# A planned attention-and-MLP kernel on one core: wq loaded by rows over two queues, Q of the first segment summed chunk by chunk, one filler, a new written-out order, the last store over two queues

## The chip, the cores and the metric

The kernel runs on one core of a Trainium2 chip. Its engines run side by side, each in its own program order: TensorE (PE, with its weight loads shown as PEld) multiplies into PSUM, VectorE (DVE), ScalarE (ACT) and GpSimd (POOL) compute on SBUF and PSUM, and SyncE (SP) issues most of the DMAs; ACT issues a few at the start. They wait for each other and for DMAs by semaphores. The metric is the device time in microseconds of one execution; lower is better. The runs of the kernel before took 265.08, 265.57 and 265.69 us, median 265.57.

## What is computed

The input x has 2048 tokens of width 512. Out comes g * A(x) + (1 - g) * B(x), where g is a sigmoid of a weighted sum of each token. A is an attention with memory over 32 heads of 16 in four segments of 512 tokens, B is a gated MLP of width 1792:

```python
q, k, v = heads(x @ wq), heads(x @ wk), heads(x @ wv)
for s in range(4):                      # segments of 512 tokens
    p = softmax(qs @ ks.T * scale + causal_mask)
    a_dot = p @ vs
    a_mem = (phi(qs) @ M) / (phi(qs) @ z + 1e-6)      # phi(t) = t + 1 if t > 0 else exp(t)
    o[s] = sigmoid(beta) * a_mem + (1 - sigmoid(beta)) * a_dot
    M, z = M + phi(ks).T @ vs, z + phi(ks).sum()
a = o @ wo
b = (relu(x @ W_gate) * (x @ W_up)) @ W_down
out = g * a + (1 - g) * b,  g = sigmoid((x * gate_w).sum(-1))
```

## The kernel before

**Tasks and a written-out order.** The kernel first describes its work as tasks (class `Plan`), each with an engine, a duration that the planner books for it in ns, the tasks that it depends on, and the PSUM banks and ring buffers that it needs and frees. `ORDER` is a list of task numbers and `UNITS` one digit per buffer slot: both were worked out ahead, outside the kernel, from the booked durations and the arrival times in `LANDS` (line 258, ns after the start). In the program they only fix in which order each engine's instructions stand and which bank each task uses. At run time an engine takes its instructions in that order and waits for what it really needs. A DMA issue waits in addition until the DMA eight issues before it, whose semaphore it uses again, has landed.

**The head.** Weights and x come by DMAs issued at the start. The four x tiles of segment 0 (128 tokens each, L266) go alternately over SP and ACT; so do the four 128-row pieces of wq (`load_wq`, L300: even ones on SP, odd ones on ACT). Then SP issues wk in two halves of 256 rows, wv, W_gate and W_up in pieces, gate_w and beta (L308, L310), and the rest. While these come in, PE runs seven matmuls on a constant (`heat`, L911), turns the x tiles (`x0_tasks`, L497: 16 matmuls of 128 columns with an identity, "flips"), whose results DVE and ACT copy from PSUM to xT (L505), and then three fillers (L515) on a tile of zeros.

**Q of segment 0** (`proj_q`, lines 542 to 551): for each of four column groups c, an accumulation in one bank over four row chunks of wq. Chunks 0 and 1 are taken together for the first half of the tokens (256 columns), then together for the second half; chunks 2 and 3 follow with 512 columns. The first half needs the x tiles 0 and 1, the second tiles 2 and 3.

**What follows, per segment.** K and V are projected in the same way (L460 is the helper that records whole matmuls, L464 the same cut into four 32-column parts, which is taken where the array is in that shape already). DVE evicts Q (L556) and K ("ktr", L572), makes masked copies of K ("KT", L575) and phi(K) ("pkT", L529, L530); ACT does the exp for phi (L534). Scores (L623, diagonal blocks L636) of four heads fill the banks 0 to 3, one ACT exp empties them (L645), GpSimd masks the result (L674), and PE multiplies it with V (L696). V is evicted by DVE or ACT (L602). The MLP (`ffn_tasks`) runs between: W_gate and W_up matmuls, relu on ACT (L860), product on DVE (L866, "hT"). `out_tile` sums W_down and wo matmuls into one bank per 128 tokens, DVE scales it (L892) and SP stores it (L897). The last tile is stored in two halves of the columns; its second half is cut into two evictions and one store.

**The head gates.** `head_gates` (lines 382 to 395) is some thirty small DVE instructions that turn beta into per-head factors, after one ACT exp of betab (L395). It is one task, booked with 2000 ns:

```python
got_eb = plan.add("ACT", 200, 0.0, lambda: nc.scalar.activation(
    eb[:], betab[:], ACT.Exp, scale=-1.0), [got_be], 100)
got_gates = plan.add("DVE", 2000, 0.0, head_gates, [got_eb], 100, lock=True)
```

Of the kernel before, what the change touches and what calls it, by code (L numbers as in the profile page):

```python
# [12 lines left out]
P = 128  # L13
# [6 lines left out]
L = S // NSEG  # L20
# [72 lines left out]
"""  # L93

UNITS = (
    "456701230142303000031221111122121222030000003000000010011000002300020000230113110223100023"
    "135121300042016323701290018020d320a211b001c00111002222003003111322000222203122100214567302"
    "1000003300000003201100000200003000001011303031023221103821070016002332053209102a3224113b02"
    "1d213c011211002010120122032121202030212232003145670132000002200000003301100000010000000033"
    "01101302038322101272209312232232036211a0115110b3024103d022c1002120132212242202021113315302"  # L100
    "135671032000002300000002301100000320000000120110238012130303027200901220233212600053214300"
    "a302d024b211c01101200110"
)


class Slot:


    def __init__(self, cands):
        self.cands, self.units, self.left = tuple(cands), (), 0  # L110

    @property
# [66 lines left out]
def kernel(  # L179
# [74 lines left out]
    def work():  # L254
        return plan.one("ps", range(7, -1, -1))


    LANDS = dict(n0=3600, n1=3800, n2=4300, n3=4450, qa=5100, qb=5900, ka=7250, kb=8550, v=10050,
                 g0=11550, u0=13000, gw=14400, be=14650, g1=15900, u1=17250, x1=20700, g2=22000,
                 u2=23100, g3=24200, u3=25300, d0=28100, d1=30800, o=33600)  # L260

# [141 lines left out]
    def K(unit, part=0.0):  # L403
        return unit * UNIT + part
# [572 lines left out]
```

## Time and profile before

| What | Value |
|---|---|
| Median of three runs | 265.57 us (265.08 to 265.69) |
| The profiled execution | 264.89 us, of which the span from first to last instruction is 263.2 us |
| PE busy | 255.8 us, 97% of the span |
| DVE, ACT, POOL busy | 204.4, 183.2, 61.9 us |
| Granted TensorE clock | 1.00 throughout |
| PE busy in 0 to 5.69 us, 5.69 to 22.8, 22.8 to 260.4 | 4.77, 16.27, 234.78 us |
| DVE busy in the same stretches | 1.94, 14.78, 187.36 us |

The span is shorter than the execution's time by what lies before the first and behind the last instruction of the program, 1.69 us. An engine's busy time counts its instructions alone. Matmuls are pipelined, so that the end of one lies behind the start of the next: the step from start to start is what one costs. A few matmul records are missing (28 of 3969 here), so a gap may be one unseen matmul. Chain and waits name who released whom by the semaphores.

### The profile page before, as it was taken

The numbers are of one execution on the slowest core, as the hardware profiler recorded it, in microseconds if no ns is written. First come the engines' busy times: TensorE is split into PE (matmuls) and PEld (weight loads), VectorE is DVE, ScalarE is ACT, GpSimd is POOL, SyncE is SP. The second block draws the span as 40 slices with busy tenths as digits, with TensorE's granted clock in tenths as the row PEclk, the third lists the DMA queues.
The fourth block names the chain that finished last, engine by engine and source line by source line (L and its number), as shares of the span: only waits on it lengthen the run. The fifth ranks groups of instructions, "written<-read, shape, count | busy, mean of one in ns | idle before, by whom it ended". The sixth has DMA issues, their size and how long they took to land.

```text
span 263.2 us, 9091 instructions
## 1 busy us (share of the span) xinstructions
PE 255.8 (97%) x3941; PEld 118.8 (45%) x3969; DVE 204.4 (78%) x473; ACT 183.2 (70%) x168; POOL 61.9 (24%) x168
## 2 busy tenths in 40 slices
PE   8999999999999999999999999999999999999995
PEld 5434444454444444444444444444444444445454
DVE  3799899999655985688998687785999767878722
ACT  3298988899777778878668667788568667873000
POOL 8022622312321322132021222122122223121000
PEclk9999999999999999999999999999999999999999
DMA  6999893011501112002204110022020100041011
GB/s 205 305 254 345 236 221 40 4 22 34 92 17 40 22 32 82 22 12 82 80 4 61 35 24 21 22 94 89 4 80 24 35 4 22 12 146 49 2 42 42
DMA packets 30031, 19.48 MB, mean 74 GB/s; under 512 B 15016, under 2 KB 28456, under 8 KB 29992
## 3 DMA queue, kind: packets, MB, share of 16 engines
q1 hardware_dynamic: 29416, 18.38, 26.0%
q8 instruction: 31, 0.51, 0.8%
q10 hardware_dynamic: 576, 0.52, 0.6%
q14 instruction: 8, 0.07, 0.1%
HBM read 13.21 MB, written 2.55 MB: 60 GB/s over the span
## 4 chain that ended last, share of the span: by engine, by line
PE 90%; DVE 4%; DMA 3%; issue 1%; SPq 0%; DVEq 0%
PE ps L460 48%; PE ps L464 24%; PE ps L623 8%; PE ps L696 7%; DMA wv_sb<-in_A_wv_dram 2%; DMA xn<-in_A_x_dram 1%; PE ps L636 1%; PE ps L816 1%; DVE KT L575 1%; DVE ktr L572 1%; DVE junk L414 1%; PE ps L752 1%; DVE hT L866 0%; DVE gcat L391 0%; PE ps L792 0%
## 5 line engine op out<-in xcount | busy, mean ns | idle before, releaser
L645 ACT ACTIVATE E<-ps 128x2048 bf16<-128x2048 f32 x64 | 120.1, 1876 | 31.3 <-PE ps L623 27.1
L674 POOL TENSOR_SCALAR_AFFINE_SELECT E<-E 128x256 bf16<-128x256 bf16 x128 | 52.6, 435 | 171.5 <-ACT E L645 171.4
L866 DVE TENSOR_TENSOR hT<-ps,rgr 128x512 bf16<-128x512 f32 x56 | 37.6, 678 | 13.4 <-PE ps L460 8.3
L860 ACT ACTIVATE rgr<-ps 128x512 bf16<-128x512 f32 x56 | 33.0, 597 | 14.7 <-PE ps L460 7.3
L460 PE MATMUL ps<-xT,wg_sb 128*128 128x512 bf16 x144 | 40.6, 380 | 1.0 <-issue 0.5
L460 PE MATMUL ps<-wd_sb,hT 128*128 128x512 bf16 (+1 forms) x161 | 37.8, 352 | 0.5 <-issue 0.5
L460 PE MATMUL ps<-xT,wu_sb 128*128 128x512 bf16 x133 | 36.4, 380 | 0.6 <-issue 0.5
L727 DVE STREAM_TRANSPOSE T<-ps 128x512 f32<-128x512 f32 x32 | 22.8, 712 | 12.0 <-PE ps L696 11.8
L623 PE MATMUL ps<-QT,KT 32*128 32x320 bf16 (+3 forms) x512 | 25.4, 273 | 0.0
L892 DVE TENSOR_SCALAR osr<-ps,ngcol 128x512 bf16<-128x512 f32 (+2 forms) x18 | 12.2, 677 | 14.7 <-PE ps L464 8.2
L464 PE MATMUL ps<-xT,wu_sb 128*32 128x512 bf16 x336 | 23.5, 379 | 0.0
L460 PEld LDWEIGHTS <-wg_sb 128*128 128x128 bf16 x152 | 13.9, 98 | 17.7 <-issue 2.4
L460 PEld LDWEIGHTS <-hT 128*128 128x128 bf16 x167 | 14.2, 98 | 16.0 <-issue 2.7
L460 PEld LDWEIGHTS <-wu_sb 128*128 128x128 bf16 x140 | 12.9, 98 | 16.1 <-issue 1.9
L464 PE MATMUL ps<-wd_sb,hT 128*32 128x512 bf16 (+1 forms) x340 | 20.0, 362 | 0.0
L623 PEld LDWEIGHTS <-KT 32*128 32x128 bf16 x512 | 7.6, 92 | 26.4 <-issue 25.9
L696 PE MATMUL ps<-E,Vp 128*17 128x320 bf16 (+3 forms) x512 | 19.5, 274 | 0.0
L464 PE MATMUL ps<-xT,wg_sb 128*32 128x512 bf16 x288 | 19.2, 379 | 0.0
L460 PE MATMUL ps<-xT,wq_sb 128*128 128x512 bf16 (+1 forms) x69 | 17.2, 355 | 0.3 <-issue 0.2
L645 ACT ACTIVATE Em<-ps 128x2048 bf16<-128x2048 f32 x8 | 15.1, 1882 | 3.3 <-PE ps L636 3.3
L460 PE MATMUL ps<-wv_sb,xT 128*128 128x512 bf16 x55 | 15.5, 379 | 0.6 <-DMA wv_sb<-in_A_wv_dram 0.6
L460 PE MATMUL ps<-xT,wk_sb 128*128 128x512 bf16 x50 | 14.3, 380 | 0.1
(102 smaller groups left out, 305.5 us busy)
## 6 DMA issues: line engine op xcount, KB each, us to landing
out_dram<-osr SPq DMA_DIRECT2D x15, 128.0 KB
wd_sb<-in_B_W_down_dram SPq DMA_DIRECT2D x2, 896.0 KB
xn<-in_A_x_dram SPq DMA_DIRECT2D x3, 512.0 KB
cdr<-coefs SPq DMA_DIRECT2D x6, 256.0 KB
xn<-coefs SPq DMA_DIRECT2D x6, 256.0 KB
wg_sb<-in_B_W_gate_dram SPq DMA_DIRECT2D x2, 512.0 KB
wu_sb<-in_B_W_up_dram SPq DMA_DIRECT2D x2, 512.0 KB
wg_sb<-in_B_W_gate_dram SPq DMA_DIRECT2D x2, 384.0 KB
```

Of the source, the lines that this page charges most:

```text
L414: zs.append(plan.add("DVE", 690, key, lambda t=t: nc.vector.scalar_tensor_tensor(junk[:], xn[:, t, :], 1.0, gwb[:], ALU.mult, ALU.mult, ac ...
L460: nc.tensor.matmul(out, lhsT=lhsT, rhs=rhs, start=start, stop=stop)
L464: nc.tensor.matmul(out[r], lhsT=lhsT[:, r], rhs=rhs, start=start, stop=stop, tile_position=(0, 32 * j))
L572: d = plan.add("DVE", 600, key - RQK, lambda: nc.vector.tensor_copy(ktr[ks.i][:], bank(sl)), [a], DVL + 40, need=[ks], frees=[sl])
L623: nc.tensor.matmul(ps[:, j * L + o:j * L + o + L - q], lhsT=KT[i][rows, kb, 3 * r:3 * r + 2].rearrange("p h q -> p (h q)"), rhs=QT[i][rows ...
L645: last_exp[0] = [plan.add("ACT", 66 + 4 * L / 1.2, key, lambda: nc.scalar.activation(dst, ps[:, 0:4 * L], ACT.Exp, scale=SCALE), [a] + war ...
L674: nc.gpsimd.affine_select(out=m[:, :, o:o + HP], in_=m[:, :, o:o + HP], compare_op=ALU.is_ge, fill=0.0, base=HP, pattern=[[0, 4], [1, HP]] ...
L696: nc.tensor.matmul(bank(sl)[32 * m:32 * m + HW, q:q + w], lhsT=(Vp[i] if n < 4 else Vm)[:, kb, r, 4 * c + j, 0:HW], rhs=rhs, start=(n == 0 ...
L727: done.append(plan.add("DVE", 633, key - RL, lambda r=r, sl=sl: nc.vector.transpose(T[ts.i][:, r], bank(sl)), [a] + done, 75 if r else 0, ...
L860: r = plan.add("ACT", 478, key - RL, lambda sl=gsl, rs=rs: nc.scalar.activation(rgr[rs.i][:], bank(sl), ACT.Relu), [g], ACL, frees=[gsl])
L866: nc.vector.tensor_tensor(hT[hs1.i][:], bank(sl), rgr[rs.i][:], ALU.mult)),
L892: nc.vector.tensor_scalar(osr[os.i][:, n0 - c0:n1 - c0], bank(sl)[:, 0:n1 - n0], ngcol[:, tt:tt + 1], None, ALU.mult)),
```

## The change

1. **wq by rows.** The first two chunks of wq (rows 0-127 and 128-255) are each halved by rows, 64 on SP and 64 on ACT, chunk 0 first on both queues. Rows 256 to 511 come in one DMA on SP. So SP issues one transfer more ahead of wk than it did with x and wq, and ACT issues two halves where it issued two whole pieces.
2. **Q of segment 0 chunk by chunk.** Four tasks (chunk 0 first half, chunk 0 second half, chunk 1 first half, chunk 1 second half), each waiting for its own chunk, and then chunks 2 and 3 as before.
3. **One filler** instead of three.
4. **Booked times.** `LANDS` names q0, q1 and qb and moves several arrivals; flips, heat and recall are booked with other durations. The head gates stay at 2000.
5. **A new ORDER and UNITS** for all tasks, from one end of the program to the other. Both programs hold the same matmuls except for two fillers.
6. **The last store** goes half by SP (64 partitions) and half by ACT.

```diff
-    LANDS = dict(n0=3600, n1=3800, n2=4300, n3=4450, qa=5100, qb=5900, ka=7250, kb=8550, v=10050,
-                 g0=11550, u0=13000, gw=14400, be=14650, g1=15900, u1=17250, x1=20700, g2=22000,
+    LANDS = dict(n0=3570, n1=3700, n2=4200, n3=4400, q0=5300, q1=5750, qb=6600, ka=7400, kb=8800,
+                 v=10500, g0=11900, u0=13100, gw=14400, be=14650, g1=15900, u1=17250, x1=20700,
...
-    def load_wq(i):
-        for ci in (2 * i, 2 * i + 1):
-            (nc.scalar if ci % 2 else nc.sync).dma_start(
-                out=wq_sb[:, ci, :], in_=A_wq[ci * P:(ci + 1) * P, :])
-        return arrival("q" + "ab"[i])
-
-    got_q = [load_wq(i) for i in range(2)]
-    got_k = [load_rows(wk_sb, A_wk, i, "k") for i in range(2)]
+    got_q = []
+    for ci in range(2):
+        for n, eng in ((0, nc.sync), (P // 2, nc.scalar)):
+            eng.dma_start(out=wq_sb[n:n + P // 2, ci, :],
+                          in_=A_wq[ci * P + n:ci * P + n + P // 2, :])
+        got_q.append(arrival("q%d" % ci))
+    got_q.append(load_rows(nc.sync, wq_sb, A_wq, 1, "q"))
+    got_k = [load_rows(nc.sync, wk_sb, A_wk, i, "k") for i in range(2)]
...
-            a = plan.add("PE", 107.0 * (c1 - c0), K(-9) + n, flip, [got_n[0][t]], PEL, need=[sl],
+            a = plan.add("PE", 80.0 * (c1 - c0), K(-9) + n, flip, [got_n[0][t]], PEL, need=[sl],
...
-                    for h in range(3):
-                        nc.tensor.matmul(bank(js)[:, 0:2 * P], lhsT=junk[:, 0:P],
-                                         rhs=junk[:, None, 0:P].to_broadcast([P, 2, P]), start=True,
-                                         stop=True)
-                j = plan.add("PE", 640, K(-9) + n + 0.5, idle, [a], lat=0, need=[js], frees=[js],
+                    nc.tensor.matmul(bank(js)[:, 0:2 * P], lhsT=junk[:, 0:P],
+                                     rhs=junk[:, None, 0:P].to_broadcast([P, 2, P]), start=True,
+                                     stop=True)
+                j = plan.add("PE", 320, K(-9) + n + 0.5, idle, [a], lat=0, need=[js], frees=[js],
...
-            for h in range(2):
-                a = matmuls(K(-8 + h, c), [got_q[0]], sl, [
+            for n, (ci, h) in enumerate(((0, 0), (0, 1), (1, 0), (1, 1))):
+                a = matmuls(K(-8 + n, c), [got_q[ci]] + (got_x[0][0] if h else x0_first), sl, [
                     lambda ci=ci, h=h: (wq_sb[:, ci, c * P:(c + 1) * P],
-                                        xT[0][:, ci, h * L // 2:(h + 1) * L // 2])
-                    for ci in range(2)], width=L // 2, at=h * L // 2, prev=a, start=not h, stop=False,
-                    chunk={0: got_x[0][0] if h else x0_first})
-            a = matmuls(K(-6, c), [got_q[1]] + got_x[0][1], sl, proj_mm(wq_sb, c, 0)[2:], prev=a,
+                                        xT[0][:, ci, h * L // 2:(h + 1) * L // 2])],
+                    width=L // 2, at=h * L // 2, prev=a, start=not n, stop=False)
+            a = matmuls(K(-4, c), [got_q[2]] + got_x[0][1], sl, proj_mm(wq_sb, c, 0)[2:], prev=a,
...
-        plan.add("SP", 400, key, lambda: nc.sync.dma_start(
-            out=outf[tt * P:(tt + 1) * P, c0:c1], in_=osr[os.i][:, 0:c1 - c0]), b[-1:],
-            1400 if tt == NT - 1 else 2400, frees=[os], xfer=400.0)
+
+        def store():
+            halves = [(nc.sync, 0, P // 2), (nc.scalar, P // 2, P)]
+            for eng, p0, p1 in halves if c0 else [(nc.sync, 0, P)]:
+                eng.dma_start(out=outf[tt * P + p0:tt * P + p1, c0:c1],
+                              in_=osr[os.i][p0:p1, 0:c1 - c0])
+        plan.add("SP", 400, key, store, b[-1:], 1400 if tt == NT - 1 else 2400, frees=[os],
+                 xfer=400.0)
...
-    plan.add("PE", 3500, -1e9, heat, lat=0, need=warm, frees=warm, size=14)
+    plan.add("PE", 3570, -1e9, heat, lat=0, need=warm, frees=warm, size=14)
```

Where the new order puts things in the first 35 us, engine by engine: PE has all of Q (four column groups) and six of K's matmuls ahead of the first V matmul, where before a part of Q's group 1 stood behind it. The flips go tile by tile (0, 1, 2, 3; before 0, 1, 3, 2), and DVE copies tile 2 ahead of its half of tile 3 (before the other way). DVE has the head gates right behind the eviction of the third K group, ahead of the second V eviction (before they stood behind that group's KT copies and two of the gate sums, L414). ACT has the exp of betab ahead of the second score exp (before behind it).

More of the change, by code (lines that the diff above doesn't have):

```diff
@@ L30 @@
 ORDER = """
[62 rows of a table removed]
[63 rows of a table added]
 """
 UNITS = (
[L96 to L102, printed above, removed]
+    "456701230123406200001221131125111001330000031000000020011000002000000000230112000322100120"
+    "005111322042207113610082239321d111a203b113c01100012323003001001022212222103203230013567013"
+    "2000002300000003301100000200002000021011122200212130123b32342216201331252138211a0037200931"
+    "3d000c120111002220101011222022113032233323000145671230000003200000003301100000310003000011"
+    "0112230402231042213211a32212006122b2038313502391127123d302c1200021121303101222230202210203"
+    "10456213000000330000000220110000000000000070011103301202232112a10311214221631251038022b011"
+    "72039122c514d11000210011"
 )
@@ L255, in work @@
         return plan.one("ps", range(7, -1, -1))
-    LANDS = dict(n0=3600, n1=3800, n2=4300, n3=4450, qa=5100, qb=5900, ka=7250, kb=8550, v=10050,
-                 g0=11550, u0=13000, gw=14400, be=14650, g1=15900, u1=17250, x1=20700, g2=22000,
-                 u2=23100, g3=24200, u3=25300, d0=28100, d1=30800, o=33600)
+    LANDS = dict(n0=3570, n1=3700, n2=4200, n3=4400, q0=5300, q1=5750, qb=6600, ka=7400, kb=8800,
+                 v=10500, g0=11900, u0=13100, gw=14400, be=14650, g1=15900, u1=17250, x1=20700,
+                 g2=22000, u2=23100, g3=24200, u3=25300, d0=28100, d1=30800, o=33600)
     def arrival(name):
@@ L291, in load_x0, with load_rows @@
         return load(eng, xn[:, t, :], x[t * P:(t + 1) * P, :], "n%d" % t)
-    def load_rows(t, ap, i, name):
-        return load(nc.sync, t[:, 2 * i:2 * i + 2, :],
+    def load_rows(eng, t, ap, i, name):
+        return load(eng, t[:, 2 * i:2 * i + 2, :],
                     ap.rearrange("(c p) n -> p c n", p=P)[:, 2 * i:2 * i + 2, :], name + "ab"[i])
     got_n[0] = [load_x0(nc.scalar if t % 2 else nc.sync, t) for t in range(4)]
-    def load_wq(i):
-        for ci in (2 * i, 2 * i + 1):
-            (nc.scalar if ci % 2 else nc.sync).dma_start(
-                out=wq_sb[:, ci, :], in_=A_wq[ci * P:(ci + 1) * P, :])
-        return arrival("q" + "ab"[i])
-    got_q = [load_wq(i) for i in range(2)]
-    got_k = [load_rows(wk_sb, A_wk, i, "k") for i in range(2)]
+    got_q = []
[6 more added lines that the diff above has]
+    got_k = [load_rows(nc.sync, wk_sb, A_wk, i, "k") for i in range(2)]
     got_v = load_cols(nc.sync, wv_sb, A_wv, 0, D, "v")
@@ L513, in idle @@
                 def idle(js=js):
-                    for h in range(3):
-                        nc.tensor.matmul(bank(js)[:, 0:2 * P], lhsT=junk[:, 0:P],
-                                         rhs=junk[:, None, 0:P].to_broadcast([P, 2, P]), start=True,
-                                         stop=True)
-                j = plan.add("PE", 640, K(-9) + n + 0.5, idle, [a], lat=0, need=[js], frees=[js],
-                             size=6)
+                    nc.tensor.matmul(bank(js)[:, 0:2 * P], lhsT=junk[:, 0:P],
+                                     rhs=junk[:, None, 0:P].to_broadcast([P, 2, P]), start=True,
+                                     stop=True)
+                j = plan.add("PE", 320, K(-9) + n + 0.5, idle, [a], lat=0, need=[js], frees=[js],
+                             size=4)
             got.append(b)
@@ L795, in pe @@
                                      tile_position=(32 * j, 32 * m))
-        a = plan.add("PE", 230, key, pe, [prj["pq", seg, c] for c in range(NC)]
+        a = plan.add("PE", 266, key, pe, [prj["pq", seg, c] for c in range(NC)]
                      + [att["mbd", seg - 1]] + [(b, 3900.25) for b in loads], PEL, need=sls,
```

125 rows, old and new, of the table ORDER are left out of this document.

## The prediction

> **What bounds the kernel now.** I read the page first (busy shares, slices, chain), then the timeline of the first 24 us and of the last 25 us.
>
> ```profile
> PE 255.8 (97%) x3941; PEld 118.8 (45%) x3969; DVE 204.4 (78%) x473; ACT 183.2 (70%) x168; POOL 61.9 (24%) x168
> ...
> PE   8999999999999999999999999999999999999995
> PEld 5434444454444444444444444444444444445454
> DVE  3799899999655985688998687785999767878722
> ...
> PE 90%; DVE 4%; DMA 3%; issue 1%; SPq 0%; DVEq 0%
> ```
>
> TensorE is busy in every slice and is 90% of the chain. So the end is the sum of the matmuls plus the few places where PE waits. DVE is nearly as full in the 2nd to 10th slice (6.6 to 66 us): there a PE wait on DVE is likeliest.
>
> ```profile
> 3.57 1.71 PE L497 MATMUL ps<-ident,xn 128*128 128x128 bf16 x16
> 5.12 0.49 PE L515 MATMUL ps<-junk 128*128 128x256 bf16 x3
> 5.69 2.87 PE L460 MATMUL ps<-xT,wq_sb 128*128 128x256 bf16 x18
> ...
> 9.49 0.38 PE L460 MATMUL ps<-xT,wk_sb 128*128 128x512 bf16 x1
> 10.42 0.60 PE L460 MATMUL ps<-wv_sb,xT 128*128 128x512 bf16 x2 [0.55 <-DMA wv_sb<-in_A_wv_dram]
> ```
>
> Read the start times, since ends overlap: from start to start a warm matmul of 512 columns takes 0.216 us, one of 256 columns 0.109. The fillers (L515) are through at 5.45 and the first Q matmul starts at 5.69: 0.25 us of waiting for wq. The second waits until 5.89, 0.09 more (the landings in the trace: wq rows 0-127 at 5.65, rows 128-255 at 5.84). Before the first V matmul one matmul record is missing (0.216), so PE stands from 9.92 to 10.42, 0.50 us, until wv lands (10.37).
>
> ```profile
> 4.24 1.77 DVE L505 CAST xT<-ps 128x512 bf16<-128x512 f32 x3 [2.63 <-PE ps L497]
> ...
> 16.86 0.22 ACT L395 ACTIVATE eb<-betab 128x32 f32<-128x32 bf16 x1
> ...
> 17.53 0.38 DVE L383 TENSOR_SCALAR gall<-eb 128x32 f32<-128x32 f32 x1
> ...
> 20.83 0.68 DVE L866 TENSOR_TENSOR hT<-ps,rgr 128x512 bf16<-128x512 f32 x1
> ...
> 22.77 1.02 PE L460 MATMUL ps<-xT,wg_sb 128*128 128x512 bf16 x4 [0.19 <-DVE hT L866]
> ```
>
> These rows show the head gates (L383 to L393) holding DVE for 3.30 us (17.53 to 20.83), whereas the plan books 2.0 us for them (line 397). PSUM evictions queue behind them, and PE pays about 0.45 us between 21.1 and 22.8. After 22.8 I compared each stretch of matmuls with columns/2.4 GHz plus 0.11 us per change of array shape (as the neighbouring stretches cost) and found no further wait to the end. So from 5.69: 260.33 (last matmul's end) - 5.69 = 254.64, of which 0.09 + 0.50 + 0.45 = 1.04 waits and **253.60 work**.
>
> **The change, part by part.**
>
> *Matmuls.* I counted both programs' PE orders. The column counts weighted by shape differ by 512, which are the two dropped fillers; changes of array shape are 151 in both. 62 fewer records come of 20 matmuls issued whole instead of as four 32-column parts, and four parts cost the same (8 such records, two matmuls, every 0.43 us). So 253.60 holds from the first Q matmul on, whatever the order.
>
> *Start.* The x0 flips end as before (issue done 5.12), one filler to 5.23. wq rows 0-127, now first on both queues, would have landed by 5.65 at the latest if nothing improved; by the bytes in front (640 KB, delivered at 4.28 by the packets, last landings 0.6 to 1.1 us behind packets) at about 5.3. Then four Q matmuls on the first half of the tokens: 4 x 0.109. The fifth needs the second half, hence all of DVE's copies (L505). Their order changes: DVE now copies tile 2 whole (0.69 by the rows) before half of tile 3 (0.43). Tile 2's flips now come before tile 3's and end at 5.06; copies 5.10 to 5.79 and 5.74 to 6.16; matmul at **6.21**. So the start of Q may lie anywhere from 5.35 to 5.77 without moving anything: DVE, not wq, is what comes last. Left from there: 253.60 - 0.44 = 253.16.
>
> *To wv.* Before wv the new order has 12 narrow and 14 wide matmuls from 6.21: 12 x 0.109 + 14 x 0.216 = 4.33, so the first V matmul comes at 10.54; the old order had 0.65 us less work there, and waited. On the way each load must have landed: wq rows 256-511 at 6.97 (one 256 KB transfer, issued at 3.71 as wk's first half was; bytes in front as before, 1024 KB at 5.60, landing about 6.6), wk's halves at 8.60 and 9.03 (before: 7.59 and 8.78), wv 10.54 (10.37), W_gate 12.28 (11.87). I take no wait. Each SP issue behind the added one is 0.4 to 0.5 us later (rows of 0.39 to 0.51 us), but these queues are full: packets of wv end at 9.23, over 4 us after its issue. Bounds: 0, and 0.38 if wv lands 0.5 us later with its issue.
>
> *Behind wv, by rows.* Scores at 11.51 (KT ready 11.19). DVE: Q's chunk 1 to 11.8, pkT, ktr of chunk 2 at 12.48, two KT, V's copy at 13.78, ktr of chunk 1 from 14.63 (its matmuls end 14.60), slot to 15.24. Now the new DVE order puts the head gates here, ahead of the V copy that frees a bank for W_gate piece 1: 15.24 + 3.30 = 18.54, V copy to 19.22, PE released at 19.27. PE gets there at 18.77 (sum of prices): **wait 0.50**. Half-way on, hT1's eviction (end 23.21) holds PE another 0.10. From there I walked DVE and ACT to 34 us (each exp 1.88 us, eviction 0.61 per slot) without finding another. Cost 0.60; bounds 0 (nobody waits) to 0.90.
>
> *The last store.* DVE's final eviction, the issue and the landing lie open at the end:
>
> ```profile
> 260.36 0.35 DVE L892 TENSOR_SCALAR osr<-ps,ngcol 128x128 bf16<-128x128 f32 x1 [0.26 <-PE ps L460]
> ```
>
> The store is issued at 260.74, its packets run 261.57 to 261.92, SP sees it at 262.29. Halving the rows can save at most that packet window's half, 0.17. Against it, in each of the three head pairs issued together (x and wq), ACT's transfer landed 0.19 us after SP's. I take 0; bounds -0.17 to +0.3 (ACT's first packet came 1.51 us after issue, SP's 1.03). ACT has nothing queued behind it. "DMA: Bandwidth & Descriptors" of the Trainium skill, section "Rules for kernel authors", says not to split a transfer by partition halves, as both halves share the same engines. By that the last store gains nothing, as I take it; the pairs' rows do not test halves.
>
> *Fillers.* Dropping two frees 0.22 us that DVE's copy then takes. The new pauses (0.1 to 0.5 us before Q, up to 0.42 before 6.21) could cost the clock; but after the 0.50 us pause at 9.92 matmuls kept 0.216. So 0; if the pace halved until 4 us of work had passed, as at the start (0.107 instead of 0.056 per flip from 3.57 to 4.85, PE at work since 0.85), it would cost 2 us, which I leave to the part outside the range.
>
> **Sum.** PE's end: 6.21 + 253.16 + 0.60 = 259.97 against 260.33: 0.36 us earlier; tail 0. The span would be 262.8 instead of 263.2. The profiled execution took 264.89 (1.69 around the span), so 264.5; the median of the runs lies 0.68 above it, so 265.57 - 0.36 = **265.2**. Within 0.2% (0.53 us) a measurement of this kernel can hardly tell from no change.
>
> **Rivals.**
> 1. *PE never waits behind the gates* (for: before's order lost only 0.45 us in 250; against: my walk). Gain 0.96: 264.6. Chance 0.20.
> 2. *wv lands with its issue*, 0.5 us later (for: one issue more on SP; against: landings follow bytes). 0.38 wait, gain 0: 265.6. Chance 0.13.
> 3. *The split does nothing for wq*: rows 0-127 complete only when both old pieces did, 5.84. Q starts 5.89, the fifth matmul at 6.33: gain 0.24, 265.3. Inside the forecast's range; chance 0.07. The skill's rule on halves, cited above, would have it so.
> 4. *Slower: betab late.* ACT's exp of betab (L395) ran at 16.86, 2.3 us after betab landed (14.55). In the new order ACT reaches it at 14.65, ahead of the second score exp, and DVE's gates wait for it. Up to a landing of 14.95 it costs nothing; beyond, each 0.1 us late is 0.1 us of DVE, then PE. It takes 15.85 to lose 0.9 us and be slower by over 0.2%. For: betab's issue moves 0.4 us; against: the transfer behind it (W_gate piece 1) landed at 16.01. Price 0.9: 266.1. Chance 0.06.
> 5. *New waits past 34 us*, one or two of the 0.45 kind: gain turned into 0.1 to 0.5 loss, 265.9. For: the whole order is new; against: none in before. Chance 0.12.
>
> The forecast itself (gain 0 to 0.6) has 0.42. Faster by over 0.2%: rival 1 and a fifth of the forecast, 0.28. Slower: rival 4 and half of 5, and some of 2 with a bad store, 0.14. Within: 0.58. The range, 264.5 to 266.0, leaves out the end of rival 4 and a stall-free run with a faster store.
>
> **What would show it.** The fifth Q matmul within 0.1 us of DVE's last xT copy, near 6.2; no wait at wv, or one under 0.2; a PE wait of about 0.5 us near 18.8 to 19.3 released by DVE's V copy behind the gates; 22.8 to the end without waits; SP's last wait over 1.4 to 1.9 us after the last store's issue (1.55 before). Wrong if wq rows 256-511 or wk hold PE, if the pace of 0.109 is lost after the fillers, or if waits appear past 34 us.

## The result and the profile after

The changed kernel takes 266.62 us (median of 12 executions, 265.99 to 267.82) against 265.39 us of the kernel before on the same chip: a ratio of 1.0050, 95% interval 1.0033 to 1.0067. A second measurement beside other kernels gave 1.0041 (1.0021 to 1.0061). So the change costs 1.0 to 1.25 us; the forecast was a gain of 0.36, and its range ended at 266.0.

The profiled execution took 267.24 us with a span of 265.5 (before: 264.89 and 263.2). The page after, busy shares, slices of TensorE and DVE, and the chain:

```profile
PE 256.5 (97%) x3878; PEld 119.6 (45%) x3907; DVE 204.8 (77%) x473; ACT 183.9 (69%) x168; POOL 62.0 (23%) x168
...
PE   8899999999999999999999999999999999999994
...
DVE  3689999999858747768998768893999968777622
...
PE 90%; DMA 4%; DVE 4%; issue 1%; SPq 1%; DVEq 0%
```

The totals say nothing: TensorE is still 97% busy. Two places do. TensorE's second slice (6.6 to 13.3 us) fell from 9 to 8, and DMA's share of the chain rose from 3% to 4%. The timeline of TensorE in that stretch, where the last column names what ended an idle time:

```profile
5.38 0.60 PE L462 MATMUL ps<-xT,wq_sb 128*128 128x256 bf16 x4
6.17 2.55 PE L462 MATMUL ps<-xT,wq_sb 128*128 128x256 bf16 x16 [0.19 <-DVE xT L507]
...
9.82 0.61 PE L462 MATMUL ps<-xT,wk_sb 128*128 128x512 bf16 x2 [0.68 <-DMA wk_sb<-in_A_wk_dram]
...
11.98 1.04 PE L462 MATMUL ps<-wv_sb,xT 128*128 128x512 bf16 x4 [0.47 <-DMA wv_sb<-in_A_wv_dram]
...
20.80 1.89 PE L462 MATMUL ps<-xT,wg_sb 128*128 128x512 bf16 x8 [0.42 <-DVE Vp L602]
```

Q starts at 5.38 and its fifth matmul at 6.17, released by DVE's last copy, as forecast (6.21). Then TensorE waits for wk's second half, for wv, and behind the head gates. From start to start, less 0.216 us for each wide matmul and 0.109 for each narrow one, the waits are 0.84 (wk; landed at 9.78, before at 8.78), 0.64 (wv; 11.94, before 10.37), 0.59 and 0.20 (gates, hT1), 0.10 at 56 us and 0.41 at 100 us: 2.78 in all. (One of the 14 wide matmuls ahead of V has no record: the step of 0.325 from 10.27 to 10.59 is one narrow matmul and that one, and not a further wait for wk, as the text of e1 below takes it (0.11). The same step stands in e9 and e10, where no load was late there.) 6.17 + 253.16 of work + 2.78 = 262.11; the last matmul ended at 262.08. (The 0.41 at 100 us is not the change's: the other profiles of the new order have 0 to 0.17 there.)

The end of the timeline, and SP's wait for the last landing, with that wait in the kernel before as the last line:

```profile
262.11 0.35 DVE L892 TENSOR_SCALAR osr<-ps,ngcol 128x128 bf16<-128x128 f32 x1 [0.38 <-PE ps L462]
262.49 0.54 ACTq L901 DMA_DIRECT2D out_dram<-osr  x1
...
SPq L977 <- DMA out_dram<-osr: 1.4, 1, 1.4
...
SPq L972 <- DMA out_dram<-osr: 1.0, 1, 1.0
```

Each half store takes 0.55 us to issue (0.33 for the single store before), and the later half lands 2.06 us after its issue started (before 1.53): 0.53 more. So this execution lost 1.75 us at TensorE's end (260.33 to 262.08) and 0.53 behind it, 2.3 of span. The medians differ by half of that, since the profiled execution of after lay above its median and that of before below its own. That is why each term is now measured by itself.

### The profile page after: what moved, and what is told of

Its sections match the earlier page's. It is cut to its first block, busy times and chain, and to the rows that moved or that the text cites. A ratio compares the mean times of both kernels' runs of the same rounds, so it can differ in the third digit from the quotient of the medians.

```text
span 265.5 us, 8973 instructions
## 1 busy us (share of the span) xinstructions
PE 256.5 (97%) x3878; PEld 119.6 (45%) x3907; DVE 204.8 (77%) x473; ACT 183.9 (69%) x168; POOL 62.0 (23%) x168
## 4 chain that ended last, share of the span: by engine, by line
PE 90%; DMA 4%; DVE 4%; issue 1%; SPq 1%; DVEq 0%
PE ps L462 52%; PE ps L466 21%; PE ps L623 8%; PE ps L696 7%; DMA wv_sb<-in_A_wv_dram 3%; DMA xn<-in_A_x_dram 1%; PE ps L636 1%; PE ps L816 1%; DVE hT L866 1%; DVE gcat L393 1%; SPq L267 1%; PE ps L752 0%; DVE T L727 0%; PE ps L792 0%; DVE dnr L765 0%
## 5 line engine op out<-in xcount | busy, mean ns | idle before, releaser
L674 POOL TENSOR_SCALAR_AFFINE_SELECT E<-E 128x256 bf16<-128x256 bf16 x128 | 53.5, 441 | 176.9 <-ACT E L645 176.8
L462 PE MATMUL ps<-xT,wg_sb 128*128 128x512 bf16 x160 | 42.5, 380 | 1.1 <-issue 0.5
L462 PE MATMUL ps<-xT,wu_sb 128*128 128x512 bf16 x139 | 39.3, 380 | 0.3
L462 PE MATMUL ps<-wd_sb,hT 128*128 128x512 bf16 (+1 forms) x153 | 34.7, 350 | 0.7 <-issue 0.5
L462 PEld LDWEIGHTS <-wg_sb 128*128 128x128 bf16 x166 | 15.3, 98 | 19.8 <-issue 3.2
L466 PE MATMUL ps<-wd_sb,hT 128*32 128x512 bf16 (+1 forms) x380 | 22.9, 363 | 0.0
L466 PE MATMUL ps<-xT,wu_sb 128*32 128x512 bf16 x312 | 21.9, 379 | 0.0
L462 PEld LDWEIGHTS <-wu_sb 128*128 128x128 bf16 x146 | 13.3, 98 | 16.9 <-issue 2.5
L462 PEld LDWEIGHTS <-hT 128*128 128x128 bf16 x157 | 13.6, 98 | 14.9 <-issue 1.5
L466 PE MATMUL ps<-xT,wg_sb 128*32 128x512 bf16 x232 | 16.5, 379 | 0.0
```

Of the source, the lines that this page charges most:

```text
L462: nc.tensor.matmul(out, lhsT=lhsT, rhs=rhs, start=start, stop=stop)
L466: nc.tensor.matmul(out[r], lhsT=lhsT[:, r], rhs=rhs, start=start, stop=stop, tile_position=(0, 32 * j))
L674: nc.gpsimd.affine_select(out=m[:, :, o:o + HP], in_=m[:, :, o:o + HP], compare_op=ALU.is_ge, fill=0.0, base=HP, pattern=[[0, 4], [1, HP]] ...
```

## The experiments

Ratios are to the kernel before on the same chip, 12 executions each (9 for the changed kernel again), with 95% intervals.

### Loads: who makes wk and wv late

**Whole pieces in the changed kernel** (e1):

```
-    for ci in range(2):
-        for n, eng in ((0, nc.sync), (P // 2, nc.scalar)):
-            eng.dma_start(out=wq_sb[n:n + P // 2, ci, :],
-                          in_=A_wq[ci * P + n:ci * P + n + P // 2, :])
-        got_q.append(arrival("q%d" % ci))
-    got_q.append(load_rows(nc.sync, wq_sb, A_wq, 1, "q"))
+    for ci in range(4):
+        (nc.scalar if ci % 2 else nc.sync).dma_start(
+            out=wq_sb[:, ci, :], in_=A_wq[ci * P:(ci + 1) * P, :])
+    got_q = [arrival(k) for k in ("q0", "q1", "qb")]
```

> The changed kernel with wq loaded as before: four whole pieces of 128 rows, alternating between SP and ACT. In the changed kernel's profile wk's second half landed at 9.78 us and wv at 11.94, against 8.78 and 10.37 before, and PE waited 0.84, 0.11 and 0.64 us for them. Theory A (the new wq pieces make the loads behind them late): wk's second half lands near 8.8 and wv near 10.4 again, these waits shrink to 0.2 or less, and the time falls by 1.2 us or more against the changed kernel, to 0.999 to 1.001 of the kernel before. Theory B (the late landings were chance in one execution): the landings may lie anywhere between, and the time stays at that of the changed kernel, 1.004 to 1.006 of before.

Measured: 266.04 us, 1.0017 (0.9999 to 1.0036). wk's second half landed at 9.34, wv at 10.77; TensorE waited 0.45 us for wk and nothing for wv. That is 0.6 us less than the changed kernel, half of what theory A expected: the loads are one cause, not the only one.

**The changed loads in the kernel before** (e4), the same edit the other way round, on the old order:

> The kernel before with the changed kernel's wq pieces (64-row halves of the first 256 rows on both queues, then 256 rows in one piece on SP) and nothing else of the change. Theory A (these pieces make the loads behind late): wk's second half near 9.8, wv near 11.9, PE waits for them about 1.5 to 2 us in sum instead of 0.5; time 1.0 to 1.6 us above before, ratio 1.004 to 1.006. Theory B (chance): landings as before, ratio 0.999 to 1.001.

Measured: 266.29 us, 1.0023 (1.0004 to 1.0042). wv landed at 11.30; TensorE waited 1.16 us for it and 0.22 for wk, against 0.50 before, and Q's start gained 0.17 but then waited 0.31. The delay goes with the loads, whatever the order. Its price, 0.9 us by the medians and 0.6 by the ratio, lies below the range given.

**What in the loads?** The program has eight semaphores for transfers in turn, so the ninth transfer is issued only when the first has landed; in every profile that is at 3.5 to 3.8 us, when the first transfer, an x0 tile, is in. Before, the first eight (x0, wq) held 1024 KB. In the changed kernel the two extra halves fill places, so that rows 256-511 of wq became the ninth. SP's issues show it; the kernel before first, then the changed one, each with its last issue ahead of the stop and the ninth transfer behind it:

```profile
1.72 0.90 SPq L300 DMA_DIRECT2D wq_sb<-in_A_wq_dram  x2
3.71 0.91 SPq L266 DMA_DIRECT2D wk_sb<-in_A_wk_dram  x2
...
1.72 1.20 SPq L303 DMA_DIRECT2D wq_sb<-in_A_wq_dram  x2
3.65 0.40 SPq L267 DMA_DIRECT2D wq_sb<-in_A_wq_dram  x1
4.09 0.99 SPq L267 DMA_DIRECT2D wk_sb<-in_A_wk_dram  x2
```

Two kernels part this from the halves themselves. e7 keeps one pair of halves but loads rows 128-255 in one piece; e8 has no halves, but two tiny loads that fill places (shown are the new lines that issue loads):

```
e7:
+    for n, eng in ((0, nc.sync), (P // 2, nc.scalar)):
+        eng.dma_start(out=wq_sb[n:n + P // 2, 0, :], in_=A_wq[n:n + P // 2, :])
+    nc.scalar.dma_start(out=wq_sb[:, 1, :], in_=A_wq[P:2 * P, :])
...
e8:
+    for ci in range(2):
+        (nc.scalar if ci % 2 else nc.sync).dma_start(
+            out=wq_sb[:, ci, :], in_=A_wq[ci * P:(ci + 1) * P, :])
...
+    for n in range(2):
+        (nc.scalar if n % 2 else nc.sync).dma_start(out=tiny[0:16, n, :], in_=x[0:16, 0:16])
```

> The changed kernel with rows 0-127 of wq in two halves, but rows 128-255 in one piece on ACT. The first eight transfers then hold 1024 KB, as before the change; in the changed kernel they hold 768 KB, and the ninth (rows 256-511) is issued only when the first x0 tile has landed (3.65 us). Theory A1 (the ninth transfer waits for the first to land, so 256 KB less are under way from 3.7 to 5 us): 1024 KB are delivered at 5.35 to 5.6 us as with whole pieces, rows 256-511 are issued near 2.9 instead of 3.65, wk's second half lands at 8.8 to 9.4, wv at 10.4 to 10.8; time 0.4 to 0.8 us below the changed kernel. Theory A2 (halves of 64 rows move slowly in themselves): half of the delay stays, 1024 KB at 5.7 or later, wv near 11.1.

> The changed kernel with rows 0-127 and 128-255 of wq in whole pieces, and behind them two loads of 512 bytes that nobody reads, so that rows 256-511 are again the ninth transfer. Theory A1 (ninth waits for the first to land): the ninth is issued at 3.65, 1024 KB are delivered at 5.9 to 6.0 us, wv lands at 11.0 to 11.9, time as the changed kernel's (266.4 to 266.8). Theory A2 (halves are slow): 1024 KB at 5.35 to 5.6, wv at 10.4 to 10.8, time 266.0.

Timelines of SP's issues and of TensorE's first V matmuls; e7 first:

```profile
2.33 0.58 SPq L267 DMA_DIRECT2D wq_sb<-in_A_wq_dram  x1
3.78 0.89 SPq L267 DMA_DIRECT2D wk_sb<-in_A_wk_dram  x2
...
10.76 1.04 PE L461 MATMUL ps<-wv_sb,xT 128*128 128x512 bf16 x4
```

and e8:

```profile
2.19 0.43 SPq L307 DMA_DIRECT2D tiny<-in_A_x_dram  x1
3.53 0.41 SPq L267 DMA_DIRECT2D wq_sb<-in_A_wq_dram  x1
3.98 0.99 SPq L267 DMA_DIRECT2D wk_sb<-in_A_wk_dram  x2
...
11.61 1.04 PE L464 MATMUL ps<-wv_sb,xT 128*128 128x512 bf16 x4 [0.29 <-DMA wv_sb<-in_A_wv_dram]
```

In e7 rows 256-511 (L267) go out at 2.33 and V starts at 10.76; in e8, without a single half, they go out at 3.53 and TensorE waits for wv. Side by side (GB/s: mean of 3.75 to 7.5 us in the DMA view):

| kernel | wq pieces | in the first eight | GB/s | wk, 2nd half | wv | ratio (interval) |
|---|---|---|---|---|---|---|
| before | whole | 1024 KB | 273 | 8.78 | 10.37 | 1 |
| e1 | whole | 1024 KB | 276 | 9.34 | 10.77 | 1.0017 (0.9999-1.0036) |
| e7 | one pair of halves | 1024 KB | 286 | 8.39 | 10.71 | 1.0016 (1.0003-1.0029) |
| e8 | whole, tiny loads | 769 KB | 257 | 9.59 | 11.56 | 1.0033 (1.0016-1.0051) |
| changed | halves | 768 KB | 232 | 9.78 | 11.94 | 1.0050 (1.0033-1.0067) |
| changed again | halves | 768 KB | 241 | 8.95 | 11.66 | 1.0041 (1.0021-1.0061) |

A1 fits, the places and not the halves: e7 is as fast as e1, e8 nearly as slow as the changed kernel (and 0.5 us above e7 on the same chip). Over all 14 profiles wv landed at 10.37 to 11.19 (mean 10.66) in the eight with 1024 KB in the first eight transfers, at 11.04 to 11.94 (mean 11.56) in the six others: 0.9 us. One mark missed: 1024 KB were delivered at 5.90 in e7, where A1 said 5.35 to 5.6 and A2 5.7 or later; from 3.75 to 5.25 us e7 moved 207 GB/s, no more than the six (171 to 213). It had caught up by 1536 KB, all that lies in front of wv (7.49; before 7.59, changed 8.33).

One thing these runs do not part. With a place used up, 256 KB are missing in front, and wk and wv also go out one SP issue later: wv at 4.47 to 4.77 us in the eight profiles, at 5.01 to 5.17 in the six, 0.44 in the mean. The 1536 KB in front of it are delivered 0.58 later in the mean (7.12 to 7.87 against 7.84 to 8.33). No kernel here takes away the bytes and keeps the issue times, so how the 0.9 us divide between the two is open.

**The changed kernel again** (e10), to see how far one profile can be trusted:

> The changed kernel again, beside the others on one chip. If the late landings come of its loads: wk's second half at 9.0 us or later, wv at 11.0 or later, store 2.05 us from issue to landing, ratio to before 1.004 to 1.006. If its first profile was chance: wv at 10.4 to 10.8, ratio still 1.004 to 1.006 by other terms.

Measured 266.53 us, 1.0041. wv at 11.66, last store 2.13 us; but TensorE now waited 0.53 for wq's rows 256-511 (landed at 7.17), nothing for wk and 0.91 for wv. Which load is late changes, that one is late does not.

### The last store

**One piece in the changed kernel** (e2), **two halves in the kernel before** (e11, the reverse edit there); e2's edit:

```
-            halves = [(nc.sync, 0, P // 2), (nc.scalar, P // 2, P)]
-            for eng, p0, p1 in halves if c0 else [(nc.sync, 0, P)]:
-                eng.dma_start(out=outf[tt * P + p0:tt * P + p1, c0:c1],
-                              in_=osr[os.i][p0:p1, 0:c1 - c0])
+            nc.sync.dma_start(out=outf[tt * P:(tt + 1) * P, c0:c1], in_=osr[os.i][:, 0:c1 - c0])
```

> The changed kernel with the last store in one piece on SP. In the changed kernel's profile the last store took 2.06 us from issue to landing, against 1.53 before. If the two half stores cost this: issue to landing 1.5 us again, time 0.5 us below the changed kernel, ratio to the kernel before about 1.003. If that was chance in one execution: ratio 1.005.

> The kernel before with the last store in two halves of 64 rows over SP and ACT and nothing else. If the split itself costs: issue to last landing 2.05 us instead of 1.53, time 0.5 to 0.6 us above before, ratio 1.002. If it costs only where ACT or SP is busy in the new order: 1.5 us, ratio 1.000.

e2: 266.04 us, 1.0019 (1.0000 to 1.0038), store 1.54 us. e11: 265.95 us, 1.0020 (1.0003 to 1.0037), store 2.13 us. The end of e11's timeline, where nothing else differs from the kernel before:

```profile
260.95 0.35 DVE L892 TENSOR_SCALAR osr<-ps,ngcol 128x128 bf16<-128x128 f32 x1 [0.26 <-PE ps L460]
261.33 0.55 SPq L900 DMA_DIRECT2D out_dram<-osr  x1
261.33 0.56 ACTq L900 DMA_DIRECT2D out_dram<-osr  x1
```

Issue 0.55 instead of 0.33; in the packets of the trace the first one came 1.19 (SP) and 1.46 us (ACT) after the issue began, instead of 0.83, and the packets of each half still took 0.31 us, where those of the whole store took 0.36. The later half landed 2.02 to 2.13 us after issue in all seven profiles with halves, the single store 1.52 to 1.54 in all seven without. The split costs 0.5 us wherever it stands.

### The order alone, and the head gates

**Whole pieces and one store** (e5, and e12 beside the changed kernel): what remains is the new order and the single filler.

> The changed kernel with wq in whole pieces and the last store in one piece: what is left of the change is the new order and the dropped fillers. With whole pieces and with one store the changed kernel each came to 266.04 us against 266.62. If the two costs add up: 265.4 to 265.5 us, ratio to the kernel before 1.000, the gates wait at 19 us (0.59) the largest wait left, and no gain from the order. If both single results saw the same thing or chance: 266.0, ratio 1.002.

> The kernel with whole pieces and one last store again (new order, one filler, nothing else of the change), now beside the changed kernel on one chip. From its first run: ratio to before 0.998 to 0.999, 1.2 to 1.5 us below the changed kernel. If the sum of the two costs was overstated there: 1.000 to 1.001. In its first profile PE's clock turned to full speed only at 6.5 us (4.5 to 5.3 in most others), 0.65 us of the start; if one filler makes that likelier it shows again here.

265.16 us, 0.9984 (0.9970 to 0.9998), and 265.36 us, 1.0000 (0.9985 to 1.0016). So the two costs make up the whole loss: 1.5 us lie between e5 and the changed kernel, 1.2 between e12 and the changed kernel beside it on one chip. Alone the order is worth 0.2 to 0.5 us by the medians (forecast 0.36), which the second interval does not tell from nothing.

**Gates on GpSimd** (e3 in the changed kernel, e6 in the order-only kernel): the copies leave head_gates for a function that is called behind task 136, GpSimd's fourth mask, and the two products that read them follow task 50.

```
-            nc.vector.tensor_copy(gcat[rows, 1], g[rows, 1, :, m])
+            nc.gpsimd.tensor_copy(gcat[rows, 1], g[rows, 1, :, m])
             for c in range(NC):
-                nc.vector.tensor_copy(gcat[rows, 0, c], g[rows, 0, c, (m + c) % 4])
+                nc.gpsimd.tensor_copy(gcat[rows, 0, c], g[rows, 0, c, (m + c) % 4])
...
+        if t.n == 136:
+            late_gates()
...
```

> The changed kernel with the twenty small copies of the head gates on GpSimd behind its fourth mask (26 to 29.3 us, idle there), the two products behind them on DVE later; the first three DVE instructions stay. DVE is held 0.9 us instead of 3.3 near 17 us. If the gates cause PE's wait at 20.0 us (0.59): that wait is gone, time 0.5 to 0.6 us below the changed kernel, ratio to before about 1.003. Rival (DVE is full for 40 us, so the wait comes again at a later eviction): 0 to 0.2 us, ratio 1.004 to 1.005.

> As the order-only kernel, and the gates' twenty small copies on GpSimd behind its fourth mask. With halves and the split store this move took PE's waits at 20 and 24 us away, but PE lost 0.66 and 0.27 us at 40 and 45 us, where DVE stood for the load of segment 1's x (issued at 33.4, landed at 37.2). If that load was late because of the loads at the start (its issue stands behind theirs on SP; it was at 32.76 with whole pieces), the wait at 40 shrinks with whole pieces and the time falls 0.3 to 0.6 us below the order-only kernel, ratio 0.998 to 0.999. If the load's latency sets it in any case, 0 to 0.2 us.

e3: 266.81 us, 1.0058 (1.0038 to 1.0077); e6: 265.58 us, 0.9991 (0.9976 to 1.0006). No gain in either (e6 lies 0.4 us above e5 by the medians, on one chip), though the waits at 20 and 24 us are gone. e6's timeline of SP, DVE and TensorE shows where they went:

```profile
34.02 0.51 SPq L277 DMA_DIRECT2D xn<-in_A_x_dram  x1
...
37.92 0.69 DVE L418 SCALAR_TENSOR_TENSOR junk<-xn,gwb 128x512 bf16<-128x512 bf16 x1 [1.99 <-DMA xn<-in_A_x_dram]
...
39.28 0.59 PE L464 MATMUL ps<-xT,wg_sb 128*128 128x512 bf16 x2 [0.29 <-DVE ktr L574]
40.98 0.59 PE L464 MATMUL ps<-xT,wu_sb 128*128 128x512 bf16 x2 [1.11 <-DVE Vp L604]
```

DVE works in order. It stood 1.99 us for segment 1's x (L277, issued on SP behind a K transpose of 1.27 us), and the evictions that TensorE needs stood behind it. In the first profile of the changed kernel (its L416 at 38.06) DVE came there so late that it did not wait; in the second (e10) it stood 0.42 us for x, which landed at 38.28, and in e5 0.45 us, with the gates still on DVE. By the steps of the 64 score exps against e12, which did not wait there, each of these two lost some 0.5 us on TensorE's side between 41 and 47 us. So what is won before 38 us is given back here, unless x lands earlier, as in e1 (36.88), which lost nothing.

**x earlier** (e9): e6 with that load (task 348) ahead of the K transpose (task 65) in SP's order.

```
-    138 421 422 124 367 123 243 40 244 248 139 423 149 418 150 245 368 65 234 140 258 43 369
-    235 348 44 259 80 151 236 152 260 141 46 370 372 153 679 45 419 371 249 49 143 250 420 142
+    138 421 422 124 367 123 243 40 244 248 139 423 149 418 150 245 368 348 65 234 140 258 43 369
+    235 44 259 80 151 236 152 260 141 46 370 372 153 679 45 419 371 249 49 143 250 420 142
```

> The kernel with whole pieces, one last store and the gates' copies on GpSimd, and segment 1's x load issued on SP ahead of the first K transpose instead of behind it. Without this move the load was issued at 34.0 us, DVE stood for it at 37 to 38 us and PE waited 1.26 us at 39.5 and 0.36 at 38.6, so that nothing was left of the 0.85 us which the gates' move had saved. Theory C (the load of segment 1's x holds everything to about 41 us, so an early gain is given back there): issue near 32.6, landing 1.4 us earlier, these waits under 0.4 in sum, time 0.5 to 1.0 us below the kernels without the move: 264.2 to 264.8 where before is 265.4. Rival (something else of DVE's queue holds PE at 40): waits over 1 us again, time 265.2 to 265.6.

```profile
31.67 0.39 SPq L277 DMA_DIRECT2D xn<-in_A_x_dram  x1
32.10 2.53 SPq L590 DMA_TRANSPOSE pK<-pkT  x2
...
36.02 0.68 DVE L418 SCALAR_TENSOR_TENSOR junk<-xn,gwb 128x512 bf16<-128x512 bf16 x1
...
39.54 0.59 PE L464 MATMUL ps<-xT,wu_sb 128*128 128x512 bf16 x2
```

264.57 us (264.05 to 265.14), 0.9971 (0.9957 to 0.9986): theory C, and the fastest kernel here, 0.8 (by the ratio) to 1.0 us (by the medians) below the kernel before. DVE takes up x without a stop, and TensorE has no wait between 5.96 and 43 us. The early x load with the gates left on DVE was not tried.

## Why the prediction was wrong, point by point

- **Work, start: right.** The fifth Q matmul came at 6.17 (6.21 forecast), released by DVE, and 253.16 us of work from there and the waits above leave 0.03 us of the end unexplained. wq's first rows landed at 5.28 (5.3 forecast).
- **"To wv. I take no wait", "but these queues are full": the step that failed.** I looked at SP's issue times and bytes and took the queue for full. It was full before because eight transfers with 1024 KB were out before the first wait for a landing. The split puts 768 KB there, and from 3.75 to 7.5 us the transfers move 232 to 257 GB/s instead of 255 to 317. The forecast's "bytes in front as before, 1024 KB at 5.60" became 5.95, and the 1536 KB in front of wv came at 8.33 instead of 7.59. wk and wv landed 1.0 and 1.6 us later in this profile (0.9 for wv in the mean), and TensorE waited 0.84 and 0.64 us for them instead of not at all. Rival 2 had the place; its 0.5 us of later issue is there (0.44 in the mean), but it is about half of the lateness, and it had nothing for wk. It was to be read before: wk's first issue, the ninth, stands at 3.71, right behind the first landing, though SP was free from 2.62. Price by the medians: 0.6 us (e1, e7), 0.9 in the old order (e4).
- **"The last store. I take 0; bounds -0.17 to +0.3": the second step that failed,** in size and beyond its bounds: +0.5. The bound came from pairs of whole loads, where the second queue landed 0.19 later, and such pairs say nothing of halves; halves issued together take 0.22 us longer to issue and start their packets 0.4 to 0.6 us later. The Trainium skill ("DMA: Bandwidth & Descriptors", "Rules for kernel authors") advises against partition halves since both share the same engines; the runs agree that nothing is won, and the loss of 0.5 us goes beyond it.
- **Head gates, 0.50 + 0.10: right in place, near in size** (0.59 + 0.20). But I ended the walk at 34 us, four short of the next bound. Taken alone the term is worth nothing (e3, e6), since x at 38 us would have cost as much; together with x it is worth 0.6 (e9 against e5, another chip) to 0.8 (against e12, the same chip). Rival 1's 264.6 is met only by e9, which also has whole pieces, one store and the early x, so the number is not that rival's.
- **Fillers, rivals 3, 4, 5.** Whether the halves helped wq's first rows is not shown: 5.28 against 5.65 in these two profiles, but 5.21 to 5.59 in the six with halves and 4.96 to 6.32 in the eight with whole pieces; rival 3 stays open. betab landed at 15.41, past the 14.95 of rival 4, but all loads of that part were late, and the gates' wait on TensorE was as long in e5 (0.59), where betab landed at 14.61. Rival 5 came true in part: past 34 us the waits of this profile were small (0.10) or not repeated (0.41), but x's load cost some 0.5 us in the changed kernel's second profile.

So the sum was 0.36 gain; with loads +0.6 to +0.9 and store +0.5 instead of 0 it is 0.7 to 1.0 us slower, against 1.0 to 1.25 measured. The gates' 0.19 above forecast and x's load point the same way; the intervals of the single terms (0.4 to 0.5 us each way) leave the rest open. Not settled: whether it is the two issues at one time or the 64 rows that make the packets of a half store start late, and why wv's landing scatters by 0.8 to 0.9 us within each group. For the time of the issue the start of the kernels speaks for the rows: pairs issued side by side took 0.39 to 0.47 us with 128 rows and 0.43 to 0.45 with 16 (e8's tiny loads), the first pair with 64 rows 0.54 to 0.58.

## What to carry to other kernels

Before splitting a load, count how many transfers go out before the first wait for a landing, and how many bytes they hold: a split that uses up a place takes bytes out of the pipe and sends the next loads out later, and the price falls on loads far behind it. Here the last small store was better in one piece on one queue. And after a wait is taken away, walk each in-order engine to its next outside bound (here DVE at a load 18 us later); what was won is kept only if that bound moves too.

## What the runs showed of the hardware

- Two stores of 32 KB issued together on SP and ACT land 0.5 us later than one of 64 KB (2.02 to 2.13 against 1.52 to 1.54 us, seven profiles each).
- At the start, loads of 64 rows issued side by side on SP and ACT took 0.54 to 0.87 us each to issue, loads of 128 rows 0.39 to 0.47. Behind a pair of halves whole pieces were slow too (0.58 and 0.84 in e7).
- A transfer reports in sixteen parts, and the last may be far behind: in e12 fourteen parts of wv were in at 9.51, the last at 11.19.
- TensorE's clock turned to full speed at 3.54 to 6.80 us in 13 profiles, with one filler and with three (6.80: e11, three fillers). When late, Q's first matmuls took up to 0.213 us each instead of 0.109; in e5's profile (6.54) the first four cost 0.33 us more. The Trainium skill ("TensorE: Matmul & The Clock Gate", "Part 1: The HAM clock gate") explains such a spread by an activity window of about 3.4 us that runs freely; the 3.3 us between the earliest and the latest agree with that, though not with the half a microsecond of variation that it gives.
